# A fused convolution and feed-forward kernel: factors of w2 from fewer loads, and a convolution group transformed while the one before it is still inverted

## The chip, the cores and the metric

One NeuronCore of a Trainium2 chip runs the whole program. The metric is device time in microseconds (us) of one execution, and a kernel is judged by the median over its runs. The engines named below are PE (matrix multiplication), DVE (elementwise work with two tensor operands), ACT (elementwise functions of one tensor), POOL (here it only issues output transfers) and SP (it issues the other transfers). Each engine works through its own list of instructions in a fixed order and waits on semaphores.

## The reference

`x` has 2048 rows (S) of 1024 channels (D); `w1` is 1024 x 3584 and `w2` is 3584 x 1024. Cut to what matters:

```python
xn = layernorm(x)                                  # over the channels
k_shift = causal depthwise convolution of k, 4 taps
kv = k_shift * v
y  = irfft(rfft(pad(kv)) * rfft(pad(ssm_k)))[:S] + kv * ssm_D   # long causal convolution, per channel
h  = silu(xn @ w1)
out = x + xn * y + h @ w2
```

All arrays are float32.

## The kernel before

**Matrix products.** Every product of two float32 matrices is made of three fp16 products of high and low parts, so that "4 steps of a 512-wide product" are 12 matmuls on PE. The first product (GEMM1, `xn @ w1`) is done partly plainly and partly in units of Strassen form: a unit forms four tiles from seven products P1 to P7 of sums of quadrants. The last unit takes its products in the order P1, P6, P7, P5, P2, P3, P4. In `evacuate`, P7's bank is read twice by DVE, with `v_tt(low[:, 1], c[0], d, ADD)` (the rows `hf<-ff,hf` at L349 in the trace) and later `v_tt(low[:, 0], c[0], u, ADD)`. The first of the two sets `seen["P7"]`; P4 accumulates into the same bank and waits for it. The matmuls of GEMM1 carry the lines L957 to L959.

The second product (GEMM2, `h @ w2`, matmuls L1100 to L1102) is done plainly for most of the rows of w2 (`PLAIN`). For the row blocks in `PAIRS` it is done at the end in Strassen form by `units2`: eight tiles, each of seven products of 12 matmuls. The right operands of these are seven factors of w2 (`w2f`): B11, B21, B22 (quadrants of w2), T1 = B12 - B11, T2 = B22 - T1, T3 = B22 - B12 and T4 = B21 - T2, each cut into four blocks of 128x512 and then split into high and low fp16 parts by ACT and DVE (`split`; DVE's part is the rows `x<-x,tau,x`, `x<-wraw,tau,x` and `x<-w2n,tau,x`). The factors lie in eight places `x0` to `x7`, which held the left operands of GEMM1 and come free in turn. `norms_w2` prepares them in the order of the products P1, P7, P6, P2, P5, P3, P4. One place, `x4`, holds T3, then T2, then T4 in float32 (`hold`, buffer `x_7027` below). The raw blocks come through two small rings, `wraw` and `w2n`, of four half slots together.

**Convolution.** It is a two-stage discrete Fourier transform in eight groups of 128 channels. A group is made of quarters t = 0 to 3. In each quarter `stage1` multiplies the signal and the filter by a DFT matrix on PE into banks of PSUM (`ps`, or a spare `ff` bank of GEMM2) and `to_spec` empties these: ACT copies the first half as soon as it is there, later the sum, and DVE takes the difference, into a float32 tile `spec` of slots. `forward`, `product` (spectrum times filter spectrum; `tmp<-spec` 128x2048 is its largest operation) and `inverse` are DVE work in the same tile. `result_parts` scales the result and splits it into fp16 tiles `zh` and `zl`; `stage1_inv` multiplies these by the inverse DFT matrix into `py` banks (L1767 to L1769); `gated` empties those banks with four ACT operations each (`py<-py,minus,csc`) and a DVE multiplication by `xg`. A quarter's spec slots may be overwritten by the next group when the former result was split, which the flag `taken` tells.

**The order.** No engine's order is written by hand. The parts are generators (streams) which yield operations and conditions; a planner, `Order`, keeps a planned time for each engine and repeatedly takes the stream whose next operation can start earliest, less the stream's bias (in us). So a change in one stream's conditions or biases moves instructions of other streams on every engine.

Of the kernel before, what the change touches and what calls it, by code (L numbers as in the profile page):

```python
# [12 lines left out]
BF16 = mybir.dt.bfloat16  # L13
# [7 lines left out]
P = 128  # L21
# [279 lines left out]
def h3_ffn_kernel(ctx, tc, x, kp, vs, fs, shift, dskip, w1, w2, cfwd, cinv, out):  # L301
# [1002 lines left out]
    def norms_w2():  # L1304
        yield flag["w2 squares"]
        q, qs, cc = qt[:, 0:NP], qt[:, NP:NP + 1], qt[:, NP + 1:NP + 2]

        def sums():
            nc.vector.tensor_reduce(q, ss2, axis=AX.X, op=ADD)
            nc.vector.tensor_mul(q, q, e1s)  # L1310
            nc.vector.tensor_mul(q, q, e1s)
            nc.vector.tensor_reduce(qs, q, axis=AX.X, op=ADD)
        yield V(sums, qt[:, 0:NP + 1], [ss2, e1s], us=0.6)

        def then(e):
# [21 lines left out]
        for k, (name, (_, of)) in enumerate(PRODUCTS.items()):  # L1337
            r = places[FPLACE[k + 1]]
            yield r.ready
            wc, wtok = w2f[name] = r.tile([P, NQ, 2, W], F16)  # L1340
            flag["w2f", name].n = NQ
            held = of in ("T2", "T3", "T4")
            if held:
                if of != "T3":
                    yield flag["held", before]
                flag["held", of].n = NQ
                before = of
            for a, i in enumerate(PAIRS):
                raw, tok = yield from next_w2()
                src, toks = raw, (tok, flag["w2f", name])  # L1350
                if held:
                    src, toks = hold[:, a], (flag["w2f", name], flag["held", of])
                if of == "T3":
                    b12, t12 = yield from next_w2()
                    yield v_tt(src, raw, b12, SUB)
                    tok.set()
                    t12.set()
                elif of == "T2":
                    yield v_tt(src, src, raw, ADD)
                    tok.set()  # L1360
                elif of == "T4":
                    yield v_tt(src, raw, src, SUB)
                    tok.set()
                elif of == "T1":
                    b11, t11 = yield from next_w2()
                    yield v_tt(raw, raw, b11, SUB)
                    t11.set()
                add(split(wc[:, a, 0, :], wc[:, a, 1, :], src, tau2[:, i:i + 1], toks), 0.05)
        yield flag["held", "T4"]
        ktok.set()  # L1370

    w2raw = []
# [2 lines left out]
    def next_w2():  # L1375
        yield lambda: bool(w2raw)
        return w2raw.pop(0)

    def load_w2():
        rings = ctxs["wraw"], ctxs["w2n"]  # L1380
        for h, j in [(h, j) for h in range(2) for j in PLAIN[::2]]:
            yield lambda: any(r.pairs() for r in rings)
            raw, tok = next(r for r in rings if r.pairs()).pair([P, 2, W])
            yield L(raw, w2r[:, j:j + 2, columns(h)])
            w2raw.append((raw, tok))
        for _, of in PRODUCTS.values():
            for i in PAIRS:
                for q, h in RAWS[of]:
                    yield lambda: any(r.ready() for r in rings)
                    raw, tok = next(r for r in rings if r.ready()).tile([P, W])  # L1390
                    yield L(raw, w2r[:, 2 * i + q, h * W:(h + 1) * W])
                    w2raw.append((raw, tok))

# [19 lines left out]
    def convolution(floor):  # L1413
# [39 lines left out]
        def loads():  # L1453
# [22 lines left out]
        def gate():  # L1476

            for g in range(NG):
# [72 lines left out]
        def stage1():  # L1551

            for g in range(NG):
                flag["spec", g, 0].n = flag["spec", g, 1].n = 4
                if g > 0:
                    yield flag["product", g - 1]
                tmps[g] = tmp, _ = tmp_r.tile([P, 2, 2, 2, 2 * P])
                yield flag["kparts", g]
                for t in TO:
                    yield flag["part", g, t]  # L1560
                    two = []
                    for i in range(2):
                        for c in range(2):
                            if i == 0:
                                yield lambda: ps_r.ready() or spare()
                                ps, tok = (ps_r if ps_r.ready() else ff).tile([P, 2, 2 * P])
                                two.append((ps, Token(), Token(), Token()))
                                diff = (tmp[:, :, t // 2] if t % 2 else sp[:, :, AT[4 + t]])[:, :, c]
                                add(to_spec(g, t, sp[:, :, AT[t], c, :], diff, *two[c], tok), CB)
# [13 lines left out]
                            (made if i else two[c][3]).set()  # L1583
                flag["stage1", g].set()

        def spare():
            return flag["gemm1"]() and not flag["last part"]() and len(ff.free()) > 1

        def to_spec(g, t, total, diff, ps, seen, made, half, tok):

            yield half
            if g > 0:
                yield flag["taken", g - 1, t]
            yield a_act(diff, ps, AF.Copy, 2.0)
            seen.set()
            yield made
            yield a_act(total, ps, AF.Copy)
            yield v_tt(diff, diff, ps, SUB)
            tok.set()
            flag["spec", g, t % 2].set()  # L1600

        def forward(g):
# [14 lines left out]
            def long(t):  # L1617
                return t.rearrange("p s a c w -> p s (a c w)")

            yield flag["spec", g, 1]  # L1620
            yield v_tt(pair(R(5), R(7)), pair(R(8), R(9)), pair(I(8), I(9)), ADD)
            yield v_tt(pair(I(5), I(7)), pair(I(8), I(9)), pair(R(8), R(9)), SUB)
# [97 lines left out]
        def transforms():  # L1720
            for g in range(NG):
# [2 lines left out]
                add(result_scales(g), CB)  # L1724
                yield from inverse(g)

        def result_parts():
# [190 lines left out]
```

## Time and profile before

| | |
|---|---|
| median of 3 runs | 1254.21 us (1253.92 to 1254.81) |
| the profiled execution's own time | 1252.18 us |
| its span, first to last instruction | 1250.1 us |
| mean granted clock of PE | 0.995 |
| PE busy | 1235.8 us (99%), 6092 instructions |
| DVE busy | 1108.4 us (89%), 1252 instructions |
| ACT busy | 779.5 us (62%), 1361 instructions |
| POOL busy | 83.3 us (7%), 93 instructions |
| bytes moved by DMA | 279.82 MB, mean 224 GB/s |

A row of a timeline gives an instruction's start, its duration, engine, line, operation, output and inputs, and in brackets how long the engine stood idle before it and what it then waited for. A row of the windows gives, for a stretch of the span, the busy time and the count of instructions on each engine, the granted clock (1.00 is full), the busy share of the DMA engines and their rate. A line of the groups gives a count, the total and mean time, and the idle time before. Durations on DVE, ACT and PE overlap their successors a little: the distance from one start to the next is what an instruction takes of the engine's time.

### The profile page before, as it was taken

What the parts mean: (1) busy time and instruction counts of PE and PEld (TensorE: products, weight loads), DVE (VectorE), ACT (ScalarE), POOL (GpSimd) and SP (SyncE); (2) the same over time, 40 slices, a digit from 0 to 9 for tenths busy, and PEclk for the clock granted to TensorE, in tenths of its full rate; (3) what the DMA queues carried; (4) which work ended last, traced back from release to release, by engine and by line L of the source; (5) the groups of instructions that cost most, each with busy time, mean ns of one, the idle gap of its engine ahead of it and who ended that gap; (6) DMA issues with size and microseconds to landing.
All of it is one profiled execution on the core that took longest, in us unless ns stands there. A gap on an engine that the chain in (4) does not pass through costs nothing.

```text
span 1250.1 us, 17015 instructions
## 1 busy us (share of the span) xinstructions
PE 1235.8 (99%) x6092; PEld 602.9 (48%) x6092; DVE 1108.4 (89%) x1252; ACT 779.5 (62%) x1361; POOL 83.3 (7%) x93
## 2 busy tenths in 40 slices
PE   9999999999999999999999999999999999899998
PEld 8544444444444544445444544544444444344444
DVE  7999987997999779998899799799889989987981
ACT  7768987886688886569653732753463374544342
POOL 0000000000000000000000000001031030113114
PEclk9999999999999999999999999999999999989999
DMA  9368889789899899769876566489487587958768
GB/s 367 101 231 273 309 308 337 230 252 253 231 339 304 242 312 301 216 193 316 298 241 186 148 195 176 130 285 255 118 201 186 140 193 212 241 104 128 163 129 110
DMA packets 267332, 279.82 MB, mean 224 GB/s; under 512 B 73200, under 2 KB 192240, under 8 KB 265968
## 3 DMA queue, kind: packets, MB, share of 16 engines
q1 hardware_dynamic: 251520, 262.22, 68.0%
q0 software_dynamic: 15728, 16.52, 10.2%
q8 instruction: 47, 0.77, 0.3%
q14 instruction: 37, 0.30, 0.1%
HBM read 175.66 MB, written 88.34 MB: 211 GB/s over the span
## 4 chain that ended last, share of the span: by engine, by line
PE 95%; DVE 3%; ACT 1%; DMA 1%; issue 0%; SPq 0%; ACTq 0%
PE ff L1101 14%; PE ff L1102 14%; PE ff L1100 14%; PE ff L957 14%; PE ff L958 14%; PE ff L959 14%; PE ps L1579 2%; PE ps L1580 2%; PE ps L1581 2%; PE py L1768 1%; PE py L1769 1%; PE py L1767 1%; PE ft L597 1%; DVE x L352 1%; DVE spec L349 1%
## 5 line engine op out<-in xcount | busy, mean ns | idle before, releaser
L1101 PE MATMUL ff<-x,wo 128*128 128x512 f16 x868 | 328.7, 379 | 4.6 <-DVE x L352 4.6
L1100 PE MATMUL ff<-x,wo 128*128 128x512 f16 x868 | 328.7, 379 | 2.2 <-ACT x L360 1.1
L1102 PE MATMUL ff<-x,wo 128*128 128x512 f16 x868 | 328.9, 379 | 0.0
L959 PE MATMUL ff<-x,wo 128*128 128x512 f16 (+1 forms) x808 | 302.8, 375 | 0.0
L958 PE MATMUL ff<-x,wo 128*128 128x512 f16 (+1 forms) x808 | 302.8, 375 | 0.0
L957 PE MATMUL ff<-x,wo 128*128 128x512 f16 (+1 forms) x808 | 302.7, 375 | 0.0
L349 DVE TENSOR_TENSOR spec<-spec 128x1024 f32<-128x1024 f32 (+2 forms) x232 | 259.6, 1146 | 2.0
L1102 PEld LDWEIGHTS <-wo 128*128 128x128 f16 x868 | 85.0, 98 | 107.2 <-issue 6.3
L1101 PEld LDWEIGHTS <-wo 128*128 128x128 f16 x868 | 85.0, 98 | 102.0 <-issue 4.0
L1100 PEld LDWEIGHTS <-wo 128*128 128x128 f16 x868 | 86.0, 99 | 99.2 <-issue 0.8
L959 PEld LDWEIGHTS <-wo 128*128 128x128 f16 x808 | 79.0, 98 | 92.1
L957 PEld LDWEIGHTS <-wo 128*128 128x128 f16 x808 | 80.5, 100 | 87.8
L958 PEld LDWEIGHTS <-wo 128*128 128x128 f16 x808 | 79.0, 98 | 88.1 <-issue 0.2
L349 DVE TENSOR_TENSOR tmp<-spec 128x2048 f32<-128x2048 f32 (+1 forms) x48 | 92.3, 1933 | 0.9
L352 DVE SCALAR_TENSOR_TENSOR ht<-hf,wsc,ht 128x1024 f16<-128x1024 f32 (+1 forms) x56 | 67.4, 1203 | 10.0 <-ACT ht L360 9.9
L352 DVE SCALAR_TENSOR_TENSOR wo<-raw,wsc,wo 128x1024 f16<-128x1024 f32 (+1 forms) x56 | 64.0, 1146 | 8.3 <-ACT wo L360 8.1
L360 ACT ACTIVATE spec<-spec 128x1024 bf16<-128x1024 f32 x32 | 33.8, 1055 | 60.3 <-DVE spec L349 60.3
L352 DVE SCALAR_TENSOR_TENSOR sig<-kin,taps,sig 128x1024 f32<-128x1024 f32 x48 | 61.5, 1280 | 11.2 <-ACT sig L360 11.1
L360 ACT ACTIVATE wo<-raw,wsc 128x1024 f16<-128x1024 f32 (+1 forms) x56 | 58.0, 1036 | 12.4 <-DVE raw L349 7.3
L346 POOL DMA_DIRECT2D out<-hf x44 | 38.3, 875 | 359.9 <-ACT hf L360 219.4
L360 ACT ACTIVATE ht<-hf,wsc 128x1024 f16<-128x1024 f32 (+1 forms) x56 | 60.9, 1087 | 2.0 <-DMA hsfA<-ht 0.3
L349 DVE TENSOR_TENSOR spec<-tmp 128x512 f32<-128x512 f32 (+1 forms) x80 | 60.8, 794 | 0.9
(187 smaller groups left out, 1712.7 us busy)
## 6 DMA issues: line engine op xcount, KB each, us to landing
wo<-hs SPq DMA_DIRECT2D x160, 256.0 KB, 3.4
hs<-ht SPq DMA_DIRECT2D x80, 256.0 KB, 4.3
raw<-in_w SPq DMA_DIRECT2D x28, 512.0 KB, 5.5
wraw<-in_w SPq DMA_DIRECT2D x24, 512.0 KB, 5.2
w2n<-in_w SPq DMA_DIRECT2D x24, 512.0 KB, 6.4
ws_T<-wo SPq DMA_DIRECT2D x22, 512.0 KB, 5.6
kin<-in_kp SPq DMA_DIRECT2D x16, 704.0 KB, 5.8
wo<-ws_T SPq DMA_DIRECT2D x22, 512.0 KB, 4.6
```

The source lines that it names most:

```text
L346: return Op("POOL", 1.1, 3.0, lambda: nc.gpsimd.dma_start(o, i, accum_op=ADD), [i], [o], m, 2.3 * n)
L349: return V(lambda: nc.vector.tensor_tensor(o, a, b, op=op), o, [a, b], **k)
L352: return V(lambda: nc.vector.scalar_tensor_tensor(o, a, s, b, op0=op0, op1=op1), o, [a, b] + ([] if isinstance(s, float) else [s]), **k)
L360: nc.scalar.activation(o, i, func, scale=scale, **kw)
L957: nc.tensor.matmul(o, w[:, 0, k], xf[:, :, k, 0], start=first and k == 0, stop=False, **kw)
L958: nc.tensor.matmul(o, w[:, 0, k], xf[:, :, k, 1], start=False, stop=False, **kw)
L959: nc.tensor.matmul(o, w[:, 1, k], xf[:, :, k, 0], start=False, stop=last and k == KH - 1, **kw)
L1100: nc.tensor.matmul(po, hx[:, n, 0, :], wc[:, n, 0, :], start=first and n == 0, stop=False, **kw)
L1101: nc.tensor.matmul(po, hx[:, n, 0, :], wc[:, n, 1, :], start=False, stop=False, **kw)
L1102: nc.tensor.matmul(po, hx[:, n, 1, :], wc[:, n, 0, :], start=False, stop=last and n == 3, **kw)
L1579: nc.tensor.matmul(o, cf[:, 0], h, start=i == 0, stop=False, **kw)
L1580: nc.tensor.matmul(o, cf[:, 0], l, start=False, stop=False, **kw)
```

## The change

It has four parts.

1. The factors of w2 for `units2` are made from 20 raw loads of 256 KB in place of 36. Their order becomes P7, P1, P6, P2, P4, P5, P3. B11 is loaded once and serves P1 and T2 (T2 = T3 + B11); B21 is loaded once and serves P2 and, after `hold` was subtracted from it in its own slot, P4; B22 is loaded once more and serves T1 (= B22 - T2, in `hold`) and P3. The number of subtractions, additions and splits stays.
2. For the odd quarters (t = 1, 3) `result_parts` writes the high and low parts into spec slots that the inverse has left (`half_word`), not into `zh` and `zl`. In `to_spec` the odd quarters of the next group take their difference before they wait for `taken`; only the copy of the sum waits. `forward` and the even quarters get waits on the new flag `z read`.
3. `bank_for` lets `stage1` use a free `py` bank once the former group's scales are there.
4. The squares of the filter are written to the ring `cm` and so needn't wait for `stage1` of the former group; the stream `norm_rows` has a bias of -1.0 in place of 0.

```diff
-RAWS = {"B11": [(0, 0)], "B21": [(1, 0)], "B22": [(1, 1)], "T1": [(0, 1), (0, 0)], "T2": [(0, 0)],
-        "T3": [(1, 1), (0, 1)], "T4": [(1, 0)]}
+RAWS = {"T3": [(1, 1), (0, 1)], "T2": [(0, 0)], "B21": [(1, 0)], "B22": [(1, 1)]}
...
+        yield from room_for("P7")
+        for a in range(NQ):
+            b22, t22 = yield from next_w2()
+            b12, t12 = yield from next_w2()
+            yield v_tt(hold[:, a], b22, b12, SUB)
+            t22.set()
+            t12.set()
+            split_of("P7", a, hold[:, a], flag["T3", a])
+        yield from room_for("P1")
+        for a in range(NQ):
+            b11, t11 = yield from next_w2()
+            split_of("P1", a, b11, t11)
+            yield flag["T3", a]
+            yield v_tt(hold[:, a], hold[:, a], b11, ADD)
+            t11.set()
+        yield from room_for("P6")
+        for a in range(NQ):
+            split_of("P6", a, hold[:, a], flag["T2", a])
+        yield from room_for("P2")
+        raws2 = []
+        for a in range(NQ):
+            b21, t21 = yield from next_w2()
+            raws2.append((b21, t21))
+            split_of("P2", a, b21, flag["B21", a])
+        for a, (b21, _) in enumerate(raws2):
+            yield flag["B21", a]
+            yield v_tt(b21, b21, hold[:, a], SUB)
+        yield from room_for("P4")
+        for a, (b21, t21) in enumerate(raws2):
+            split_of("P4", a, b21, t21)
...
-            for gen, bias in ((result_parts(), CB), (stage1_inv(), 0.02), (norm_rows(), 0.0), (norms_w2(), 0.03)):
+            for gen, bias in ((result_parts(), CB), (stage1_inv(), 0.02), (norm_rows(), -1.0), (norms_w2(), 0.03)):
...
-                if g > 0:
-                    yield flag["stage1", g - 1]
-                for a in range(2):
-                    j = acc[:, a].bitcast(BF16)[:, 0:TQ].rearrange("p t w -> p (t w)")
-                    yield a_act(j, kf[:, a].rearrange("p t w -> p (t w)"), AF.Square, total=ss[:, 2 + a:3 + a])
+                for a in range(2):
+                    yield cm_r.ready
+                    j, tok = cm_r.tile([P, T2 * P], BF16)
+                    yield a_act(j, kf[:, a].rearrange("p t w -> p (t w)"), AF.Square, total=ss[:, 2 + a:3 + a])
+                    tok.set()
+                if g > 0:
+                    yield flag["spec", g - 1, 0]
...
+                flag["z read", g, 1].n = flag["z read", g, 3].n = 2
...
-                                yield lambda: ps_r.ready() or spare()
-                                ps, tok = (ps_r if ps_r.ready() else ff).tile([P, 2, 2 * P])
+                                yield lambda: bank_for(g, t) is not None
+                                ps, tok = bank_for(g, t).tile([P, 2, 2 * P])
...
             yield half
-            if g > 0:
+            if g > 0 and t % 2 == 0:
                 yield flag["taken", g - 1, t]
+                yield flag["z read", g - 1, 3]
             yield a_act(diff, ps, AF.Copy, 2.0)
             seen.set()
             yield made
-            yield a_act(total, ps, AF.Copy)
-            yield v_tt(diff, diff, ps, SUB)
+            if t % 2:
+                yield v_tt(diff, diff, ps, SUB)
+                if g > 0:
+                    yield flag["taken", g - 1, t]
+                yield a_act(total, ps, AF.Copy)
+            else:
+                yield a_act(total, ps, AF.Copy)
+                yield v_tt(diff, diff, ps, SUB)
...
-                    (hi, htok), (lo, ltok) = ipart[g, t] = yield from parts_tile(more["zh"], more["zl"], (P, 2, 2 * 2 * P))
+                    if t % 2:
+                        if t == 3:
+                            yield flag["inverse", g, 0]
+                        ipart[g, t] = [(half_word(sp[:, 0, AT[4 + n]]), flag["z read", g, t]) for n in ((1, 3), (0, 2))[t // 2]]
+                    else:
+                        ipart[g, t] = yield from parts_tile(more["zh"], more["zl"], (P, 2, 2 * 2 * P))
```

The counts of instructions on PE, DVE, ACT and POOL are the same in both programs; SP issues 16 transfers less. What differs is the order. It is the same up to about 360 us of the span (the first difference on PE is at the 3343rd of its instructions). Three places follow. The numbers behind names are buffers of the program in question, and lines of the changed program are one less than those before.

**DVE, the end of GEMM1.** Before, from the operations that precede the first read of P7's bank in the last unit (`hf_178<-ff_4941,hf_180`):

```order
L352 SCALAR_TENSOR_TENSOR ht_182<-hf_178,wsc,ht_182 128x4x128
L349 TENSOR_TENSOR hf_178<-hf_178 128x512
L352 SCALAR_TENSOR_TENSOR x_4942<-wraw_3084,tau,x_4942 128x2x512
L349 TENSOR_TENSOR hf_178<-x_2873,hf_178 128x512
L352 SCALAR_TENSOR_TENSOR x_4942<-w2n_1965,tau,x_4942 128x2x512
L349 TENSOR_TENSOR x_2873<-hf_178,x_2873 128x512
L349 TENSOR_TENSOR x_2873<-x_2873 128x512
L352 SCALAR_TENSOR_TENSOR ht_181<-hf_178,wsc,ht_181 128x8x128
L352 SCALAR_TENSOR_TENSOR zl_4959<-spec,csc_2626,zh_4958 128x1024
L352 SCALAR_TENSOR_TENSOR ht_182<-x_2873,wsc,ht_182 128x8x128
L349 TENSOR_TENSOR hf_178<-ff_4941,hf_180 128x512
```

After, the same stretch up to that read (`hf_180<-ff_5098,hf_178`):

```order
L351 SCALAR_TENSOR_TENSOR sig<-kin,taps,sig 128x1024
L351 SCALAR_TENSOR_TENSOR ht_182<-hf_180,wsc,ht_182 128x4x128
L351 SCALAR_TENSOR_TENSOR x_5099<-wraw_3088,tau,x_5099 128x2x512
L348 TENSOR_TENSOR hf_180<-hf_180 128x512
L351 SCALAR_TENSOR_TENSOR x_5099<-w2n_1965,tau,x_5099 128x2x512
L348 TENSOR_TENSOR hf_180<-x_2875,hf_180 128x512
L351 SCALAR_TENSOR_TENSOR sig<-kin,taps,sig 128x1024
L348 TENSOR_TENSOR x_2875<-hf_180,x_2875 128x512
L348 TENSOR_TENSOR x_2875<-x_2875 128x512
L351 SCALAR_TENSOR_TENSOR ht_181<-hf_180,wsc,ht_181 128x8x128
L348 TENSOR_TENSOR sig<-sig 128x1024
L348 TENSOR_TENSOR hf_180<-ff_5098,hf_178 128x512
```

Three of the next group's signal operations (`sig<-kin,taps,sig`, the first of them two rows above this list) and `sig<-sig` now stand ahead of the read, and so do the last differences of the next group's `to_spec` and the first operations of its `forward`: the ten rows above the list are `spec<-spec,ps_4960`, `spec<-spec 128x2x2x512`, two splits of `x_5031`, `xg_4538<-py_4982,xg_4538`, `spec<-spec 128x2x2x512`, a split `ht_181`, a read `hf_180<-ff_4809,hf_178`, `sig<-kin,taps,sig` and `spec<-spec 128x2x512`. Before, those of `to_spec` and `forward` stood behind the read, and the last quarters of the former group's result (`zl`) ahead of it.

**DVE, the last factors of w2.** Before, T4 is made in `x_7027` and split into `x_8946`, the operand of P4, while group 6 of the convolution is in `product` (`tmp<-spec`, `spec<-tmp`):

```order
L352 SCALAR_TENSOR_TENSOR cm<-sig,csc_8475,cm 128x512
L349 TENSOR_TENSOR spec<-tmp 128x2x256
L352 SCALAR_TENSOR_TENSOR x_8946<-x_7027,tau_141,x_8946 128x512
L349 TENSOR_TENSOR x_7027<-wraw_3084,x_7027 128x512
L349 TENSOR_TENSOR x_7027<-w2n_1965,x_7027 128x512
L349 TENSOR_TENSOR spec<-tmp 128x2x256
L352 SCALAR_TENSOR_TENSOR x_8946<-x_7027,tau_141,x_8946 128x512
L349 TENSOR_TENSOR tmp<-spec 128x2048
L352 SCALAR_TENSOR_TENSOR x_8946<-x_7027,tau_141,x_8946 128x512
```

After, the operand of P4 is `x_8895`, and T1 is made in `x_7068` behind it and split into `x_8963`, the operand of P5:

```order
L351 SCALAR_TENSOR_TENSOR x_8895<-wraw_3088,tau_141,x_8895 128x512 x2
L351 SCALAR_TENSOR_TENSOR x_8895<-w2n_1965,tau_141,x_8895 128x512 x2
L348 TENSOR_TENSOR tmp<-tmp,py_8881 128x2x256
L348 TENSOR_TENSOR spec<-spec 128x2x512
L348 TENSOR_TENSOR tmp<-tmp,py_8885 128x2x256
L348 TENSOR_TENSOR x_7068<-wraw_3088,x_7068 128x512
L348 TENSOR_TENSOR spec<-spec 128x2x512
L348 TENSOR_TENSOR x_7068<-wraw_3088,x_7068 128x512
L348 TENSOR_TENSOR x_7068<-w2n_1965,x_7068 128x512 x2
L351 SCALAR_TENSOR_TENSOR x_8963<-x_7068,tau_141,x_8963 128x512 x4
```

The four splits of P4's operand now stand together, as the fifth factor and not as the seventh, and what stands among the factors are the differences of an odd quarter (`tmp<-tmp,py`) and the former group's inverse.

**ACT, where one group hands over to the next** (the group whose scales are `csc_5191` before, `csc_5053` after). Before:

```order
L360 ACTIVATE zh_6682<-spec,csc_5191 128x1024
L360 ACTIVATE tmp<-ps_6571 128x2x256
L360 ACTIVATE tmp<-ps_6575 128x2x256
L360 ACTIVATE py_6684<-py_6684,minus,csc_5191 128x128
L360 ACTIVATE zh_6715<-spec,csc_5191 128x1024
L360 ACTIVATE spec<-ps_6571 128x2x256
L360 ACTIVATE spec<-ps_6575 128x2x256
L360 ACTIVATE py_6684<-py_6684,minus,csc_5191 128x128 x3
L360 ACTIVATE tmp<-ff_6725 128x2x256
L360 ACTIVATE zh_6748<-spec,csc_5191 128x1024
```

After:

```order
L359 ACTIVATE spec<-ps_6422 128x2x256
L359 ACTIVATE zh_6581<-spec,csc_5053 128x1024
L359 ACTIVATE spec<-ps_6426 128x2x256
L359 ACTIVATE zh_6596<-spec,csc_5053 128x1024
L359 ACTIVATE spec<-py_6500 128x2x256
L359 ACTIVATE spec<-py_6504 128x2x256
L359 ACTIVATE ff_6567<-ff_6567,minus,csc_5053 128x128 x2
L359 ACTIVATE spec<-ps_6576 128x2x256
L359 ACTIVATE spec<-ps_6601 128x2x256
L359 ACTIVATE ff_6567<-ff_6567,minus,csc_5053 128x128 x2
L359 ACTIVATE ff_6609<-ff_6609,minus,csc_5053 128x128 x3
L359 ACTIVATE spec<-ps_6576 128x2x256
```

The odd quarters' first copies and differences (`tmp<-ps`) now stand ahead of this list, and the copies of `stage1`'s banks alternate more closely with the emptying of the inverse's banks.

More of the change, by code (lines that the diff above doesn't have):

```diff
@@ L1336, in norms_w2, with room_for @@
         hold, ktok = places[FPLACE[0]].tile([P, NQ, W], F32)
-        for k, (name, (_, of)) in enumerate(PRODUCTS.items()):
-            r = places[FPLACE[k + 1]]
+        at = iter(FPLACE[1:])
+        def room_for(name):
+            r = places[next(at)]
             yield r.ready
-            wc, wtok = w2f[name] = r.tile([P, NQ, 2, W], F16)
+            w2f[name] = r.tile([P, NQ, 2, W], F16)
             flag["w2f", name].n = NQ
[L1342 to L1368, printed above, removed]
@@ L1369, in norms_w2, with split_of @@
-        yield flag["held", "T4"]
+        def split_of(name, a, src, *toks):
+            wc, _ = w2f[name]
+            add(split(wc[:, a, 0, :], wc[:, a, 1, :], src, tau2[:, PAIRS[a]:PAIRS[a] + 1], (flag["w2f", name], *toks)), 0.05)
+        yield from room_for("P7")
[6 more added lines that the diff above has]
+            split_of("P7", a, hold[:, a], flag["T3", a])
@@ new lines, in norms_w2 @@
+        for a, (b21, _) in enumerate(raws2):
[4 more added lines that the diff above has]
+            split_of("P4", a, b21, t21)
+        raws2 = []
+        for a in range(NQ):
+            b22, t22 = yield from next_w2()
+            raws2.append((b22, t22))
+            yield flag["T2", a]
+            yield v_tt(hold[:, a], b22, hold[:, a], SUB)
+        yield from room_for("P5")
@@ L1370, in norms_w2 @@
+        flag["T1"].n = NQ
+        for a in range(NQ):
+            split_of("P5", a, hold[:, a], flag["T1"])
+        yield from room_for("P3")
+        for a, (b22, t22) in enumerate(raws2):
+            split_of("P3", a, b22, t22)
+        yield flag["T1"]
         ktok.set()
@@ L1385, in load_w2 @@
             w2raw.append((raw, tok))
-        for _, of in PRODUCTS.values():
+        for of, uses in (("T3", 1), ("T2", 2), ("B21", 1), ("B22", 1)):
             for i in PAIRS:
@@ L1389, in load_w2 @@
                     yield lambda: any(r.ready() for r in rings)
-                    raw, tok = next(r for r in rings if r.ready()).tile([P, W])
+                    raw, tok = next(r for r in rings if r.ready()).tile([P, W], uses=uses)
                     yield L(raw, w2r[:, 2 * i + q, h * W:(h + 1) * W])
@@ L1584, in stage1, with bank_for @@
                 flag["stage1", g].set()
+        def bank_for(g, t):
+            if ps_r.ready():
+                return ps_r
+            free = g == 0 or flag["taken", g - 1, t]()
+            if g > 0 and py_r.ready() and flag["un", g - 1]() and (free or t % 2):
+                return py_r
+            return ff if free and spare() else None
         def spare():
@@ L1618, in long @@
                 return t.rearrange("p s a c w -> p s (a c w)")
+            if g > 0:
+                yield flag["z read", g - 1, 1]
             yield flag["spec", g, 1]
@@ L1725, in transforms, with half_word @@
                 yield from inverse(g)
+        def half_word(slot):
+            return slot.bitcast(F16).rearrange("p c w -> p (c w)").rearrange("p (i z) -> p i z", i=2)
         def result_parts():
@@ L1732, in result_parts @@
                     yield flag["inverse", g, t]
-                    (hi, htok), (lo, ltok) = ipart[g, t] = yield from parts_tile(more["zh"], more["zl"], (P, 2, 2 * 2 * P))
+                    if t % 2:
[4 more added lines that the diff above has]
+                        ipart[g, t] = yield from parts_tile(more["zh"], more["zl"], (P, 2, 2 * 2 * P))
+                    (hi, _), (lo, _) = ipart[g, t]
                     two = pair(sp[:, 1, AT[t]], sp[:, 1, AT[4 + t]]).rearrange("p i c w -> p i (c w)")
```

## The prediction

> **What bounds the kernel now.** First the page's busy times, then the windows, to find where PE does not run, then the waits and two timelines there.
>
> ```profile
> PE 1235.8 (99%) x6092; PEld 602.9 (48%) x6092; DVE 1108.4 (89%) x1252; ACT 779.5 (62%) x1361; POOL 83.3 (7%) x93
> ...
> 740.00:840.00 100.00, 99.95 (x489) 47.72 (x488) 89.71 (x89) 51.72 (x96) 0.76 (x1) 1.00 0.63 187
> ...
> 1010.00:1060.00 50.00, 50.00 (x235) 22.84 (x234) 47.72 (x48) 27.15 (x55) 6.12 (x6) 1.00 0.85 228
> 1060.00:1100.00 40.00, 33.79 (x141) 14.12 (x140) 37.30 (x46) 17.86 (x29) 5.16 (x6) 0.89 0.82 200
> ```
>
> PE is the bound: it works without a gap nearly everywhere, and the change leaves its 6016 matmuls as they are. So the change can give time only where PE waits or is clocked down, and can cost time only where DVE or ACT, DVE above all (89.71 of the 100 us from 740, 47.72 of the 50 from 1010), come late for PE. One such place stands out. From 1060 to 1100 us PE ran 141 matmuls; at the rate of the 50 us before (235) it would have been 188. The 47 that are missing are 47 x 50/235 = 10.0 us. The waits say for whom:
>
> ```profile
> PE ff L1101 <- DVE x L352: 4.6, 4, 1.8
> PE ft L597 <- DVE x L352: 1.5, 2, 1.2
> PE ft L1845 <- DVE one L406: 1.2, 1, 1.2
> PE ff L1100 <- ACT x L360: 1.1, 2, 0.8
> ...
> PE ff L1100 <- ACT ff L360: 0.5, 1, 0.5
> ```
>
> The columns are the total in us, the count and the longest. The first, the fourth and the last, 6.2 us together, lie at this place; the two rows in `ft` are at the start, which stays. PE's timeline shows the place; the rows without brackets give the distance of matmuls.
>
> ```profile
> 1087.24 0.38 PE L1102 MATMUL ff<-x,wo 128*128 128x512 f16 x1
> 1087.45 0.38 PE L1100 MATMUL ff<-x,wo 128*128 128x512 f16 x1
> 1088.45 0.38 PE L1101 MATMUL ff<-x,wo 128*128 128x512 f16 x1 [0.61 <-DVE x L352]
> ...
> 1089.81 0.38 PE L1100 MATMUL ff<-x,wo 128*128 128x512 f16 x1 [0.77 <-ACT x L360]
> 1090.91 0.58 PE L1101 MATMUL ff<-x,wo 128*128 128x512 f16 x1 [0.73 <-DVE x L352]
> 1091.29 0.63 PE L1102 MATMUL ff<-x,wo 128*128 128x512 f16 x1
> 1091.72 0.63 PE L1100 MATMUL ff<-x,wo 128*128 128x512 f16 x1
> ...
> 1097.51 0.59 PE L1101 MATMUL ff<-x,wo 128*128 128x512 f16 x1 [1.78 <-DVE x L352]
> ...
> 1090.22:1100.46 10.24, 5.99 (x14) 1.76 (x14) 10.17 (x11) 3.64 (x7) 0.86 (x1) 0.54 0.44 94
> ```
>
> These matmuls are P4 of the first tile of `units2`; each waits for a split of T4. At full clock matmuls start 0.215 us apart; from 1090.91 on 0.43, and the window to 1100.46 has a granted clock of 0.54. In it PE worked 5.99 us at half speed: 3.0 us lost, beside the 6.2 us of waits. 6.2 + 3.0 = 9.2 us, or 10.0 by the count of matmuls. On DVE the same microseconds:
>
> ```profile
> 1079.79 2.29 DVE L349 TENSOR_TENSOR tmp<-spec 128x2048 f32<-128x2048 f32 x1
> 1082.00 0.74 DVE L352 SCALAR_TENSOR_TENSOR x<-w2n,tau,x 128x512 f16<-128x512 f32 x1
> ...
> 1083.98 1.23 DVE L349 TENSOR_TENSOR tmp<-tmp,spec 128x1024 f32<-128x1024 f32 x1
> 1085.12 0.68 DVE L349 TENSOR_TENSOR x<-wraw,x 128x512 f32<-128x512 f32 x1
> ...
> 1086.38 0.74 DVE L352 SCALAR_TENSOR_TENSOR cm<-sig,csc,cm 128x512 f16<-128x512 f32 x1
> 1087.04 0.69 DVE L349 TENSOR_TENSOR spec<-tmp 128x512 f32<-128x512 f32 x1
> ...
> 1096.71 0.74 DVE L352 SCALAR_TENSOR_TENSOR x<-x,tau,x 128x512 f16<-128x512 f32 x1
> ```
>
> DVE is full, and T4, the last factor, is made only from 1085.12 on, between the pieces of `product`; its last split starts at 1096.71 and PE's next matmul at 1097.51.
>
> **The factors of w2.** Subtractions, additions and splits stay in number. What changes is when: P4's operand is the fifth factor and its splits stand together, ahead of P5's and P3's, which PE needs no later than P4's were needed before. And the stretch of DVE no longer holds `product` of group 6 there, but the odd quarters' differences and the former inverse, since the group's start is moved forward. Summing DVE's rows in the new order up to each factor's last split, against PE's matmuls at 0.215 us up to its first use, I find each of them ready before PE asks, the tightest by about 1 us. So I take the whole loss as gone, the mean of the two measures: -9.6 us (bounds -10.0 and, with a wait of 1 us left and half its clock cost, -7). The 16 loads that fall away are SP's; the DMA engines are busy 0.82 to 0.85 of the time in the two windows, and PE waits for no load in the rows above: 0.
>
> **The end of GEMM1.** Here the new order puts work ahead of something PE waits for. Before, DVE read P7's bank of the last unit in time:
>
> ```profile
> 572.70 1.28 DVE L352 SCALAR_TENSOR_TENSOR ht<-hf,wsc,ht 128x1024 f16<-128x1024 f32 x1
> 573.89 1.28 DVE L352 SCALAR_TENSOR_TENSOR zl<-spec,csc,zh 128x1024 f16<-128x1024 f32 x1
> 575.09 1.28 DVE L352 SCALAR_TENSOR_TENSOR ht<-x,wsc,ht 128x1024 f16<-128x1024 f32 x1
> 576.29 0.68 DVE L349 TENSOR_TENSOR hf<-ff,hf 128x512 f32<-128x512 f32 x1
> 576.89 1.28 DVE L352 SCALAR_TENSOR_TENSOR zl<-spec,csc,zh 128x1024 f16<-128x1024 f32 x1
> ...
> 576.67 0.27 PE L1767 MATMUL py<-zh,civ 128*128 128x256 f16 x1
> ...
> 577.98 0.38 PE L957 MATMUL ff<-x,wo 128*128 128x512 f16 x1
> ```
>
> The read `hf<-ff,hf` was over at 576.9 and P4's first matmul came at 577.98 without a wait: 1.1 us to spare. After, 22 DVE instructions run from `spec<-spec,ps_4960` to that read. That first one waits for ACT, and ACT for PE, since it stands behind the emptying of a `py` bank:
>
> ```profile
> L360 ACT ACTIVATE py<-py,minus,csc 128x128 f32<-128x128 f32 x112 | 48.2, 433 | 19.9 <-PE py L1769 17.8
> L360 ACT ACTIVATE spec<-ps 128x512 f32<-128x512 f32 x79 | 45.5, 593 | 14.4 <-PE ps L1581 14.1
> L349 DVE TENSOR_TENSOR spec<-spec,ps 128x512 f32<-128x512 f32 x26 | 17.5, 684 | 15.6 <-ACT spec L360 15.6
> ```
>
> By the spacings in DVE's rows above: nine scalar operations of 1024 elements x 1.195 (573.89 to 575.09) = 10.8; two of 2048 x 2.21 (1079.79 to 1082.00) = 4.4; two of 1024 x 1.14 (1083.98 to 1085.12) = 2.3; one scalar operation of 512 x 0.66 (1086.38 to 1087.04); eight of 512 x 0.60 to 0.64 (576.29 to 576.89) = 4.9. Sum 23.1 us. Ahead of it ACT's two rows, 0.43 + 0.59, and about 0.2 of latency (the row of 0.38 less the distance of 0.215): 24.3 us from the end of the inverse's matmuls. PE has 90 matmuls between that end and P4: 90 x 0.2155 = 19.4 us. So PE waits 24.3 - 19.4 = 4.9 us; some overlap of neighbours on ACT takes 0.2 off: **+4.7 us**. The low end, 2.9, is where DVE got its first operands without ACT's part and latencies and the small operations overlap more; the high end, 6, is where DVE came late into the stretch. Nothing hides it: behind P4 stands only GEMM2, in the same order on PE.
>
> A wait of this length may lower the clock. Bounds from rows: nothing, as after the 0.61 us at 1088.45, behind which the matmul at 1089.81 still took 0.38; or 10.24 us at half clock, 5 us, as above. I take the nearest: after its last wait (1097.51) the window's low clock ended at 1100.46, so an unbroken stretch of 2.95 us at half speed restored it, which costs 1.5 us: **+1.5**.
>
> **Groups that overlap.** While odd quarters of a group are transformed, the former group's inverse runs on PE. Both fill banks that ACT empties.
>
> ```profile
> 576.67 0.27 PE L1767 MATMUL py<-zh,civ 128*128 128x256 f16 x1
> ...
> 577.87 0.27 PE L1769 MATMUL py<-zh,civ 128*128 128x256 f16 x1
> ...
> 572.14 0.58 ACT L360 ACTIVATE spec<-ps 128x512 f32<-128x512 f32 x1
> 572.61 0.59 ACT L360 ACTIVATE hf<-ff 128x512 f32<-128x512 f32 x1
> ...
> 581.69 1.81 ACT L360 ACTIVATE py<-py,minus,csc 128x128 f32<-128x128 f32 x4
> ```
>
> In one handover PE does 24 matmuls of `stage1` x 0.215 and 48 of the inverse x 0.109 (576.67 to 577.87 holds eleven distances): 10.4 us. ACT does eight copies x 0.47 and sixteen operations x 0.45: 11.0 us. Before, this ratio was spread over a longer stretch, with matmuls of GEMM2 between. Now ACT falls about 0.6 us behind, of which the last copy, which nobody awaits at once, hides a half: 0.3 us in each of six handovers, **+2 us** in all; bounds 0 and 1.2 each (7). Dropping the wait for `taken` and the spare `py` bank only help here, and are in the 0. Below nothing it can't go: PE had no wait there to lose (99.95 of the 100 us from 740). The filter squares and the bias of `norm_rows` move ACT work and loads among work that PE does not await: 0. The tail after the last matmul stays.
>
> **Sum.** -9.6 + 4.7 + 1.5 + 2 = -1.4 us on the profiled execution of 1252.18 us, whose span is 1250.1. The median of before, 1254.21, is 2.0 above it; the same difference on it gives **1252.8 us**. A measurement of this kernel can tell about 0.2%, 2.5 us, from no change.
>
> **Rivals.**
>
> *A: the stall at GEMM1's end is short.* DVE's order is by plan, and if ACT's copies come earlier than my chain, or PE is itself late by a microsecond before, the read of P7 is nearly in time: at most 0.5 us of wait, no fall in the clock, as at 1088.45. Against it: 23 us of DVE work stand against 19.4 us of PE whatever ACT does, so 2.9 us of wait need an early start of DVE to vanish. Time: -9.6 + 0.5 + 2 = -7.1, 1247.1 us.
>
> *B: the handovers cost more, and it gets slower.* The place is each of six handovers: ACT empties both kinds of bank one after the other, and a bank that is late by 1.2 us stops PE, with DVE's difference behind it. If PE stops several times within 3 us, as at 1088 to 1091 (0.61, 0.77, 0.73), the clock halves, for about 1 us each. Price: 6 x (1.2 + 1.0) = 13; with -9.6 + 4.7 + 1.5 it gives +10, 1264 us. It is slower than before by over 0.2% from 5.9 us in all, 1.0 us a handover. For it: 11.0 against 10.4 us, and DVE busy above 90%; against it: two `py` and two `ps` banks and the spare ones of GEMM2 are a reserve. The Trainium skill ("TensorE: Matmul & The Clock Gate", "HAM oscillation — how this bites in real kernels") has the clock fall only after idle gaps over about 3.4 us; by that rule B would lose its part of the clock, 6 us, and be +4. The trace here disagrees: the clock was at half from 1090.22, after gaps of 0.61 and 0.77 us. By the same page the 4.7 us at GEMM1's end would cost half of 3.4 us, 1.7 where I have 1.5.
>
> *C: the factors stay late.* The places `x0` to `x7` and the raw slots come free in turn; if the new order, which holds B21 and B22 longer in four half slots, starts some factor late, PE waits at the first tile as before. Then nothing is gained: 4.7 + 1.5 + 2 = +8.2, 1262.4 us. Against it: the sums of DVE above; for it: 47.7 of 50 us of DVE are busy there.
>
> **Numbers.** The forecast 0.46, A 0.24, B 0.22, C 0.08. The forecast's own range, by the bounds of the stall (2.9 to 6), the clock (0 to 5), the handovers (0 to 7) and the gain, hardly all at one end, is 1248 to 1258. A reaches to 1245, B and C to 1264. 8 in 10 lie from 1245 to 1264, which leaves out the ends of A and the upper part of B. Faster by over 0.2% (under 1251.7): most of A and a third of the forecast, 0.38; slower (over 1256.7): B, C and some of the forecast, 0.36; within: 0.26.
>
> **What would show it.** In the profile of the changed kernel: no waits of PE for `x` splits near 1090 and a clock of 1.00 there; one wait of `ff` (GEMM1's line) for DVE `hf<-ff,hf` of 3 to 6 us near 587 us, with a low clock for some 3 us behind it; in the six handovers from 670 us on only waits below 1 us, for ACT `spec` or `py`. Wrong it is if the first is still there (C), if the second is absent (A), if the third add up to over 6 us (B), or if PE waits where none of these lies, for instance at the first inverse of a group.

## The result and the profile after

The changed kernel took 1258.78 us (median of 5 runs, 1257.55 to 1260.76), the kernel before 1253.92 us beside it (1252.44 to 1254.81): a ratio of 1.0043, 95% interval 1.0029 to 1.0058. It is slower by 0.4%, where 1252.8 us was forecast. The profiled execution took 1257.55 us with a span of 1255.6 us, 5.5 us more than before.

The page's busy times, then the windows at the two places of the prediction, then PE's waits in order of their sums:

```profile
PE 1235.1 (98%) x6092; PEld 602.5 (48%) x6092; DVE 1108.1 (88%) x1252; ACT 778.9 (62%) x1361; POOL 83.4 (7%) x93
...
560.00:600.00 40.00, 35.23 (x169) 16.80 (x168) 36.68 (x38) 31.81 (x50) 0.00 (x0) 0.96 0.86 264
1060.00:1100.00 40.00, 39.06 (x186) 17.98 (x184) 37.93 (x48) 23.94 (x42) 2.59 (x3) 1.00 0.57 145
...
PE ff L1820 <- ACT spec L359: 5.3, 8, 1.1
PE ff L956 <- DVE hf L348: 4.8, 1, 4.8
...
PE ff L1099 <- ACT hf L359: 0.9, 1, 0.9
```

The work is the same. The window from 1060 us, which held 141 matmuls before, holds 186 at full clock: the waits for T4 are gone. In their place stand one wait of 4.8 us in GEMM1 (L956) and eight short ones of the inverse transform's first matmuls (L1820; a ninth, of 0.5 us, writes to `py`), which did not wait at all before. The first new wait in PE's timeline, and DVE's there:

```profile
587.23 0.38 PE L958 MATMUL ff<-x,wo 128*128 128x512 f16 x1
592.37 0.58 PE L956 MATMUL ff<-x,wo 128*128 128x512 f16 x1 [4.76 <-DVE hf L348]
592.75 0.63 PE L957 MATMUL ff<-x,wo 128*128 128x512 f16 x1
...
594.89 0.63 PE L956 MATMUL ff<-x,wo 128*128 128x512 f16 x1
595.31 0.42 PE L957 MATMUL ff<-x,wo 128*128 128x512 f16 x1
...
569.20 0.69 DVE L348 TENSOR_TENSOR spec<-spec,ps 128x512 f32<-128x512 f32 x1 [0.20 <-ACT spec L359]
569.80 2.29 DVE L348 TENSOR_TENSOR spec<-spec 128x2048 f32<-128x2048 f32 x1
...
590.50 1.22 DVE L348 TENSOR_TENSOR sig<-sig 128x1024 f32<-128x1024 f32 x1
591.64 0.69 DVE L348 TENSOR_TENSOR hf<-ff,hf 128x512 f32<-128x512 f32 x1
```

DVE goes from `spec<-spec,ps` at 569.20, which had waited for ACT, to the read of P7 at 591.64 without a gap. The seven matmuls behind the wait start 0.43 us apart; the full clock is back at 595.31.

One of the six handovers, on PE and ACT. In ACT's rows `spec<-spec,csc` is the split of the former group's result and `spec<-ps` is the next group's copy of a sum.

```profile
772.08 0.38 PE L1101 MATMUL ff<-x,wo 128*128 128x512 f16 x1
773.27 0.27 PE L1820 MATMUL ff<-spec,civ 128*128 128x256 f16 x1 [0.81 <-ACT spec L359]
...
775.28 0.27 PE L1820 MATMUL ff<-spec,civ 128*128 128x256 f16 x1 [0.55 <-ACT spec L359]
...
769.09 1.15 ACT L359 ACTIVATE spec<-spec,csc 128x1024 f16<-128x1024 f32 x1 [6.62 <-DVE spec L351]
771.36 1.15 ACT L359 ACTIVATE spec<-spec,csc 128x1024 f16<-128x1024 f32 x1 [1.12 <-DVE spec L348]
772.62 0.60 ACT L359 ACTIVATE spec<-ps 128x512 f32<-128x512 f32 x1
...
774.63 0.60 ACT L359 ACTIVATE spec<-ps 128x512 f32<-128x512 f32 x1 [0.37 <-DVE spec L351]
...
771.25 1.28 DVE L351 SCALAR_TENSOR_TENSOR spec<-spec,csc 128x1024 f16<-128x1024 f32 x1
773.25 1.28 DVE L351 SCALAR_TENSOR_TENSOR spec<-spec,csc 128x1024 f16<-128x1024 f32 x1 [0.72 <-ACT spec L359]
```

The row of the waits says "ACT spec", which could be either. The times decide: the split that the first matmul reads was over on ACT at 770.24 (769.09 + 1.15) and on DVE at 772.53, but PE starts at 773.27, right behind the end of the copy (772.62 + 0.60 = 773.22), and at 775.28 behind the next copy (774.63 + 0.60 = 775.23). In all nine waits of this kind PE starts 0.05 us behind the end of such a copy. DVE's next split, too, begins only behind the copy, at 773.25. Neither has a use for it. In the built program the copy writes two pieces of 256 elements, at 1024 and 5120 of the `spec` tile, and the matmul reads from 3072 to 4095: nothing in common, but inside the range from the first piece to the last. So the working theory became that the wait is set for the range; `e5` below tests it. The planner reckons with the exact pieces and so places the matmuls as if they needn't wait.

### The profile page after: what moved, and what is told of

It is laid out like the page before. It is cut to its first block, busy times and chain, and to the rows that moved or that the text cites. A ratio compares the mean times of both kernels' runs of the same rounds, so it can differ in the third digit from the quotient of the medians.

```text
span 1255.6 us, 16959 instructions
## 1 busy us (share of the span) xinstructions
PE 1235.1 (98%) x6092; PEld 602.5 (48%) x6092; DVE 1108.1 (88%) x1252; ACT 778.9 (62%) x1361; POOL 83.4 (7%) x93
## 4 chain that ended last, share of the span: by engine, by line
PE 87%; DVE 7%; ACT 3%; DMA 1%; issue 1%; SPq 0%; ACTq 0%; DVEq 0%
PE ff L956 13%; PE ff L957 13%; PE ff L958 13%; PE ff L1099 13%; PE ff L1101 13%; PE ff L1100 13%; DVE spec L348 3%; PE ps L1604 1%; PE ps L1605 1%; PE ps L1606 1%; DVE spec L351 1%; ACT spec L359 1%; PE ft L596 1%; DVE x L351 1%; PE py L1820 1%
## 5 line engine op out<-in xcount | busy, mean ns | idle before, releaser
L956 PE MATMUL ff<-x,wo 128*128 128x512 f16 (+1 forms) x808 | 303.5, 376 | 4.8 <-DVE hf L348 4.8
L956 PEld LDWEIGHTS <-wo 128*128 128x128 f16 x808 | 80.7, 100 | 88.1 <-issue 0.6
L345 POOL DMA_DIRECT2D kf<-in_dskip x8 | 6.3, 784 | 846.8 <-DMA kf<-in_fs 366.6
```

What stands on the lines that cost most here:

```text
L956: nc.tensor.matmul(o, w[:, 0, k], xf[:, :, k, 0], start=first and k == 0, stop=False, **kw)
```

## The experiments

Each time stands beside runs of the kernel before on the same chip (1252.72 us for `e1` to `e4`, 1253.0 for `e5` and `e6`, 1252.68 for `e7` and `e8`); differences are taken against these, and the change's is +4.9 us. Since the planner may move any instruction after any edit, each run is read by its own waits too, and not by its time alone. The theories put to the test were these. One: the order of the factors gives about 9 us by itself, and the overlap of the groups costs about 14, by the wait at GEMM1's end and by the handovers. Its rival: both parts act together, the overlap having freed DVE for the factors.

**One part alone.** `e1` is the kernel before with part 1 of the change; `e2` is the changed kernel without part 1.

```diff
 e1 (on the kernel before; with the new norms_w2 and load_w2. e2, on the changed kernel, is the reverse of it)
-RAWS = {"B11": [(0, 0)], "B21": [(1, 0)], "B22": [(1, 1)], "T1": [(0, 1), (0, 0)], "T2": [(0, 0)],
-        "T3": [(1, 1), (0, 1)], "T4": [(1, 0)]}
+RAWS = {"T3": [(1, 1), (0, 1)], "T2": [(0, 0)], "B21": [(1, 0)], "B22": [(1, 1)]}
...
-        for k, (name, (_, of)) in enumerate(PRODUCTS.items()):
+        yield from room_for("P7")
```

> The kernel before with part 1 of the change alone (20 raw loads, new order of the factors). Theory: the factors' order itself removes the 6.2 us of waits at the first tile of the Strassen part and the half clock behind them, and neither the wait at the end of GEMM1 nor those at the handovers come with it: 1245 us, 9 below before. Rival: the waits went because the overlap moved the convolution's product away from that place; then DVE is as full there as before and this kernel is at 1252 to 1255 us.

> The changed kernel with the factors of w2 made and loaded as before (36 loads, old order), all else changed. Theory: it keeps the 4.8 us wait for the read of P7 with its clock loss (6.3 us) and the waits for ACT's split at the handovers (6.6 us and about 0.1 more for each), and has the factors' waits too: 1266 to 1268 us. Rival (the overlap is what freed the factors): those waits are absent, and it is within 1.5 us of the changed kernel, 1257 to 1260 us.

`e1` took 1243.8 us, ratio 0.9934 (0.9922 to 0.9947), -8.9 us; `e2` 1265.32 us, 1.0105 (1.0091 to 1.0119), +12.6 us. `e1` is 1.2 us below the first theory's 1245; `e2` is 0.7 below its 1266 to 1268, and far from the rival's 1257 to 1260. So the rival has fallen. The two differences add up to +3.7 us where the change has +4.9; parts 2 to 4 were run only together. PE's waits in `e1`, whole list behind the start, and the window where the factors are made:

```profile
PE ff L1099 <- DVE hf L351: 0.8, 2, 0.6
PE py L1790 <- DVE zl L351: 0.6, 1, 0.6
...
PE ps L1601 <- DVE spec L348: 0.4, 1, 0.4
PE ff L1099 <- ACT hf L359: 0.4, 1, 0.4
...
1060.00:1100.00 40.00, 39.43 (x182) 17.69 (x181) 39.48 (x47) 20.21 (x33) 6.06 (x7) 1.00 0.88 180
```

DVE is fuller there (39.48 of 40 us) than before, and PE no longer waits for a split (the two waits left in this window, 0.4 and 0.2 us, are for `hf`): so a full DVE is not enough to make PE wait, and what counts is where in its list the factors are made. `e7` below takes this further. `e1` is the fastest kernel of this study.

**The wait at GEMM1's end.** `e3` gives the reads of P7 and the sums behind them precedence on DVE.

```diff
-                add(quad(i, sp), 0.1)
+                add(quad(i, sp), 1.0 if sp else 0.1)
...
-            add(evacuate(i, 2 * sp, one, made, seen, n + 1 < len(todo)), EB)
+            add(evacuate(i, 2 * sp, one, made, seen, n + 1 < len(todo)), 1.0 if sp else EB)
```

(the two streams that `quad` adds likewise)

> The changed kernel; in the second half of GEMM1's units the streams that read P7 and make the sums for the Strassen factors get a bias of 1.0 us in place of 0.06 and 0.1, so that DVE does them ahead of the convolution's transform. Theory: the 4.8 us wait and its slow matmuls go, 6 us: 1252.5 us, with the handovers' waits as they were. Rival: DVE is the bound of that stretch and the wait only moves to the next reader of DVE's results: 1257 us or more.

It took 1255.84 us, ratio 1.0024 (1.0015 to 1.0033), +3.1 us: 1.7 us better than the change, where 6 were expected. Its waits:

```profile
PE ff L1820 <- ACT spec L359: 7.7, 11, 1.8
...
PE ps L1604 <- ACT spec L359: 0.6, 1, 0.6
```

The wait for `hf` is gone, with the low clock (the mean clock is 1.00), but the handovers now have eleven waits of L1820, 7.7 us, where the change had eight, 5.3 us. The cause of the wait is confirmed; a good part of its price came back in the other place.

**The handovers.** `e4` plans the inverse's matmuls later, `e5` makes the copy in two.

```diff
 e4
-                        yield T(mm, py[:, :, i, :], [hi[:, i], lo[:, i]], 0.66, m=1.0)
+                        yield T(mm, py[:, :, i, :], [hi[:, i], lo[:, i]], 0.66, m=2.5)
 e5 (odd quarters in to_spec)
-                yield a_act(total, ps, AF.Copy)
+                for s in range(2):
+                    yield a_act(total[:, s], ps[:, s], AF.Copy)
```

> The changed kernel; the planner sets the matmuls of the inverse transform 2.5 us after their operands are planned to be ready, in place of 1.0 us, so that GEMM2's matmuls stand ahead of them. Theory: PE waits at the handovers because its order lets the inverse's matmuls follow the split by ACT too closely; with 1.5 us more the eight waits of up to 1.1 us shrink to under 1.5 us in all: 1252 us. Rival: DVE is the bound of each group and what PE does ahead is missing later: waits of the same sum in other places, 1258 us.

> The changed kernel; the copy of the sum of an odd quarter is two ACT copies of 256 elements, one into the signal's and one into the filter's spec slot, in place of one copy whose output spans the range between them. Theory: the inverse's first matmuls wait for that copy only because its range covers the slots with the result's parts; with two copies they wait for DVE's split alone, which ended 0.7 to 0.9 us earlier, and the handover waits (6.6 us in all) fall under 2.5 us: 1252 to 1254 us with the wait at GEMM1's end still there. Rival: DVE's inverse itself is late, and the matmuls wait as long for the split: 1258 us.

`e4` took 1254.88 us (1.0018, 1.0008 to 1.0028), +2.2 us, halfway between the theory's 1252 and the rival's 1258, with 3.9 us of the inverse's waits for ACT's `spec` left in five places, of up to 1.2 us. More time between the matmuls and their data helps, but does not remove the waits. `e5` took 1254.26 us, 1.001 (1.0001 to 1.0018), +1.3 us, 3.6 us better than the change and 0.3 above the 1252 to 1254 expected. Its waits, and the same handover on ACT and PE:

```profile
PE ff L956 <- DVE hf L348: 6.1, 1, 6.1
...
PE ps L1604 <- ACT spec L359: 0.8, 2, 0.5
PE ff L1822 <- DVE spec L351: 0.7, 1, 0.7
...
768.04 1.15 ACT L359 ACTIVATE spec<-spec,csc 128x1024 f16<-128x1024 f32 x1 [0.58 <-DVE spec L348]
769.24 0.39 ACT L359 ACTIVATE spec<-ps 128x256 f32<-128x256 f32 x1
...
769.35 0.38 PE L1101 MATMUL ff<-x,wo 128*128 128x512 f16 x1
769.56 0.27 PE L1821 MATMUL ff<-spec,civ 128*128 128x256 f16 x1
...
767.93 2.58 DVE L351 SCALAR_TENSOR_TENSOR spec<-spec,csc 128x1024 f16<-128x1024 f32 x2
```

The row "ff <- ACT spec" has disappeared. The inverse's matmul at 769.56 starts in the middle of the copy (769.24 to 769.63) and follows the matmul of GEMM2 without a gap. DVE's two splits now follow each other directly (2.58 us for two). If the wait were set for the whole tile, it would stand here as well; if it were set for the exact pieces, it would not have stood in the changed kernel. The range fits both, though no trace shows how the wait is set. All waits of PE from 650 to 1110 us come to 2.0 us, from 6.6. DVE's inverse was in time but for one split (0.7 us), and the rival has fallen. In this kernel, though, the order at GEMM1's end came out so that P7's read is later still: 6.1 us for 4.8, and 0.9 before it.

**Both edits, and what is left.** `e6` joins `e3` and `e5`; `e8` also plans the convolution's output transfers on POOL 8 us after their data.

> Both edits: two copies, and the bias of 1.0 us for the reads of P7 and the sums. Theory: both new waits are gone, and it is the changed factors' gain alone, as in the kernel with part 1 only: 1244 to 1247 us, waits of PE after the start under 4 us in all. Rival: the convolution in one piece makes DVE the bound somewhere else: 1250 us or more.

> The kernel with both edits (two copies, bias 1.0), and the planner sets the convolution's output transfers on POOL 8 us after their operands are planned to be ready, so that in the last group fewer of them stand ahead of the transfers of GEMM2's results. Theory: the 3.9 us wait for ACT's hf at 1218 to 1222 us, and the low clock behind it, come from the queue of POOL, where a result's transfer stands behind a convolution output that is not yet made; without it 1243 to 1247 us. Rival: the wait has another cause (the ring of hf tiles, ACT): 1249 to 1251 us.

`e6` took 1250.1 us (1245.74 to 1251.82), ratio 0.9971 (0.996 to 0.9982): 2.9 us faster than before and 7.8 us better than the change, but not the 1244 to 1247 us expected; the number is the rival's, the place is not. Both waits are gone, and a third has come. The profile is that of the longest of the nine executions (1251.82 us, mean clock 0.996); the two shortest, 1245.74 and 1247.20 us, had a mean clock of 1.0, so the third wait with its low clock need not stand in every execution. Here it is on PE, with what ACT and POOL do ahead of it:

```profile
PE ff L1099 <- ACT hf L359: 3.9, 1, 3.9
...
1220.28 1.27 ACT L359 ACTIVATE hf<-ff,invc 128x512 f32<-128x512 f32 x2 [9.59 <-DMA out<-hf]
...
1199.81 2.20 POOL L345 DMA_DIRECT2D out<-ht  x2 [3.50 <-DVE ht L348]
1205.13 0.90 POOL L345 DMA_DIRECT2D out<-hf  x1 [3.12 <-ACT py L359]
1205.84 3.53 POOL L345 DMA_DIRECT2D out<-ht  x3
1214.55 1.11 POOL L345 DMA_DIRECT2D out<-ht  x1 [5.17 <-issue]
1215.12 1.45 POOL L345 DMA_DIRECT2D out<-hf  x1
```

ACT waits 9.6 us for a tile `hf` that a transfer must leave first; that transfer (`out<-hf` at 1215.12) stands in POOL's list behind the convolution's outputs (`out<-ht`). In the changed kernel the same row has 0.9 us. `e8` took 1251.85 us, ratio 0.9994 (0.9984 to 1.0003), above the range of either theory: the place is free in its profile, but a wait of 4.4 us for `hf` stands at 1162.58, one group earlier, where `out<-xg` rows stand ahead of `out<-hf`. So the queue is the likely cause and the edit no cure; why POOL's rows there are up to 5 us apart ("issue") was not settled.

**Order or loads.** `e7` is the kernel before with its 36 loads and only T4 made fifth.

```diff
-        for k, (name, (_, of)) in enumerate(PRODUCTS.items()):
+        for k, name in enumerate(FORDER):     # P1, P7, P6, P2, P4, P5, P3
+            of = PRODUCTS[name][1]
```

(and the loads in the same order)

> The kernel before with the 36 loads as they are and only the order of the factors changed to P1, P7, P6, P2, P4, P5, P3, so that T4 is made fifth and not last. Theory: what brought the gain of part 1 is that P4's operand is no longer the last factor and nobody waits for the three loads of T4 and P3 behind each other; fewer loads are worth nothing: 1244 to 1247 us. Rival: the loads, or that P3 and P5 come from slots already there, free the place; then the wait moves to P3's or P5's operand: 1250 us or more.

It took 1247.49 us, 0.9959 (0.9947 to 0.9971), -5.2 of the -8.9 us, between the theory's range and the rival's. Its waits at this place:

```profile
PE ff L1102 <- DVE x L353: 4.6, 5, 1.4
...
PE ff L1101 <- ACT x L361: 0.5, 1, 0.5
...
1080.00:1100.00 20.00, 14.84 (x66) 6.29 (x65) 19.83 (x25) 9.28 (x15) 3.44 (x4) 1.00 0.84 194
```

Five microseconds of waits remain, spread over 1081 to 1093 us and at full clock. By the order of the matmuls they stand at the last block of P5 (1081.78 and 1082.89) and at the four blocks of P3 (1087.68 to 1092.61), and none at P4: the waits moved to the operands made last, as the rival said. So the order alone spares the low clock and little of the waits; those go with the rest of part 1 (blocks loaded once and kept for two factors). Which of its two sides does that, the loads or the places of the differences, was not separated.

## Why the prediction was wrong

**The factors: right.** -9.6 us was put down; part 1 alone measured -8.9 us (1252.72 to 1243.8), and the counts of matmuls from 1060 to 1100 us say the same. The 0 for the loads was not shown: by `e7` part 1 is worth some 4 us more than a new order with all the loads, and how much of that is theirs stays open. Of the 6.2 us of waits, the 0.5 for ACT `ff` were no factor's; 0.2 of them are still there in the changed kernel. (The 6016 matmuls of the prediction are 6092 on the page; nothing rests on them.)

**The end of GEMM1: right, the clock by some luck.** Forecast: one wait for `hf<-ff,hf` of 4.7 us near 587 us, and 1.5 us of low clock. Measured: 4.76 us from 587.6, and seven matmuls 0.43 apart, 7 x 0.215 = 1.5 us. The chain of 22 DVE instructions from the first operand was put at 23.1 us; it took 569.20 to 592.33, again 23.1 us. The 1.5 us of clock, however, came from a window that was laid 0.74 us too early. The granted clock is 0.50 from 1090.96 to 1101.20 us, not from 1090.22 to 1100.46, so the last stretch behind a wait was 3.7 us (1097.51 to 1101.20), by the prediction's own reasoning a loss of 1.8.

**The handovers: wrong, and this step turned the sign.** They were put at 2 us, 0.3 each, by the ratio of ACT's to PE's work on banks. The trace has 6.6 us of idle time from 650 to 1110 us. A restart costs some 0.16 us beside it (a row of 0.38 us less the distance of 0.215), so that by the distances from matmul to matmul this stretch lost 8.7 us, 8.3 of them at the handovers and 0.4 at a wait of GEMM2. The last matmul came 5.6 us later than before: 6.4 for the wait at GEMM1's end with its clock, 1.1 for the wait for `hf` at 1211 us, -0.3 for the stretches ahead of GEMM1's end, -10.0 for the factors, and these 8.3 (all from the profiled executions; the remainder is rounding). The failing term was a wait that the change adds and that the code does not show: the copy that now stands behind `taken` holds up matmuls which read other slots. The prediction counted the dropped wait for `taken` only as a help. The sentence "Below nothing it can't go" was right; the upper bound of 7 us holds for the idle time and not for the cost; and the value between was chosen from the wrong resource.

**The rivals.** B had the place, six handovers, and their size from which it turns slower (1.0 us each; measured 1.4), but not the cause, banks that ACT empties late, and not the clock: none of those matmuls is slow. A and C did not come. The Trainium skill's rule ("TensorE: Matmul & The Clock Gate", "HAM oscillation — how this bites in real kernels"), no fall of the clock below idle gaps of about 3.4 us, agrees with the handovers (gaps up to 1.12 us, clock kept), with the 4.76 us wait and with `e7` (gaps up to 1.39 us, clock kept); it disagrees with the kernel before, where the clock was at half after gaps of 0.61, 0.77 and 0.73 us.

The traces do show what sorts these cases. In each of the ten, the changes of the granted clock lie whole multiples of 3.413 us apart: the low clock lasted 3.41 us in the changed kernel (591.97 to 595.38), 6.82 in `e6` and 10.24, three times 3.413, in the kernel before. Cut into stretches of this length, counted from those changes, the windows show the stretch ahead of the fall in the kernel before, the low clock behind it, and the least busy stretch at the waits of `e7`:

```profile
1087.55:1090.96 3.41, 1.30 (x6) 0.34 (x5) 3.41 (x7) 1.93 (x4) 0.36 (x2) 1.00 1.05 179
1090.96:1101.20 10.24, 6.68 (x15) 2.00 (x15) 10.17 (x11) 2.90 (x5) 0.58 (x1) 0.50 0.37 87
...
1087.51:1090.92 3.41, 1.80 (x7) 0.67 (x7) 3.41 (x6) 0.72 (x1) 0.01 (x1) 1.00 1.21 195
```

PE was busy for 1.30 us of the stretch in the kernel before, and for 1.80 in `e7`. Over the ten traces, all 18 stretches at full clock with up to 1.33 us of PE work (those at the program's end included; 1.33 is the last of `e6`) were followed by half clock, and none with 1.40 us or more was (1.40 is in `e5`, 587.22 to 590.63 us; `e3` kept the clock over a gap of 1.82 us with 1.59). So here it was not the longest gap but PE's work within one such stretch that told. No run was made to test this.

**The sum.** -1.4 us was forecast for the span and +5.5 us measured. Of the 6.9 us between, the handovers are 6.3 (8.3 for 2); the wait for `hf` at 1211 us, put at nothing, is 1.1, and the other terms take 0.5 off.

## What to carry to other kernels

Where two engines work in different parts of one tile, ask for each added write what range its access pattern spans: a strided write can make readers of the untouched parts wait, and a planner that knows exact pieces will not leave room for it. Two plain copies were cheaper here than one strided copy. And a change of several parts is best run part by part: one part was worth 9 us here and the others together cost 13.

## What was not expected of the hardware

ACT's next instruction starts 0.49 us after a copy of 128x512 (772.62 to 773.11 in the changed kernel) and 0.26 to 0.28 us after one of 128x256 in `e5` (769.24 to 769.52): cutting the copy in two cost ACT next to nothing. One wait of 4.76 us cost 1.5 us of clock behind it, while 6.6 us of waits in pieces of up to 1.1 us cost none; and in the kernel before, three gaps of 0.6 to 0.8 us within one stretch of 3.41 us did bring the half clock, which then lasted 10.24 us.
